# Tile-by-tile first products and a split MLP norm in a fused local-attention and MLP kernel

## The chip, the cores and the metric

The kernel runs on one core of a Trainium2 chip. The metric is the device time of one launch in microseconds. TensorE is PE (its weight loads are PEld), VectorE is DVE, ScalarE is ACT, GpSimd is POOL, and SyncE is SP, which here only issues DMAs. ACT and POOL issue some DMAs too.

## What is computed

The input is one sequence of 2048 rows of 512 features in bf16. It is normalised, goes through an attention with 32 heads of 16 features, in which each row sees eight earlier rows at a distance of two, and through an MLP block with shifted features. Their product is added to the input. Cut to its core:

```python
xn = layernorm(x)
# branch A: q, k, v = split(xn @ wqkv); row i sees rows i, i-2, ..., i-14
s  = concat_heads(softmax(q . k[i - 2w] * 16 ** -0.5, over w = 0..7) . v[i - 2w]) @ wo
# branch B: D = 512, F = 1376
h  = gelu(layernorm(xn) @ w1)            # features in four groups of 128,
hs = shift_rows(h, +1, -1, +2, -2) @ w2  # each group shifted by its own number of rows
x1 = xn + hs
b  = x1 + gelu(layernorm(x1) @ w3) @ w4
out = x + s * silu(b)
```

## The kernel before

**Layout.** Rows are split by parity, p = 0 for the even rows and p = 1 for the odd ones, so that "every second row" becomes "neighbouring rows". Each parity has 1024 rows, in two chunks of 512: chunks 0 and 1 are the even rows, 2 and 3 the odd ones. A chunk is four tiles of 128 rows. `xn[p]` holds rows on partitions, `xnT[p]` features on partitions, which is what the products need.

**Order.** The whole program is written out by hand from line 760 on, under a manual schedule: every engine takes its instructions in the order of the source lines, and waits in that order. So the place of a call in the list sets its place in five queues at once, and an instruction that waits holds back all that are behind it on its engine.

**The head** (lines 763 to 849). SP loads chunk 0 tile by tile, then the q and k weights in two DMAs (lines 140 and 141, 512 KB each), then chunk 1, `w1`, chunks 2 and 3, `wv` and `w2`. For chunk 0 each tile goes through

- `ln_first` (304): statistics on DVE (`bn_stats`, `bn_aggr`, an addition of eps), and the inverse root as a power on POOL (315),
- `first_n` (317): the normalisation on DVE,
- `first_t` (324): four PE transposes into PSUM and a copy by ACT to `xnT`.

`qk_pair(c, a, halves)` (423) makes 256 of the q and k features of a chunk in one double bank of PSUM, which ACT copies out. For chunk 0 the first three pairs run in two halves of 256 rows: the first half of each between the transposes, the second halves later. `warm` (173) is a product without use that keeps PE running.

The second norm of a chunk (branch B normalises the already normalised rows) is not computed on the rows: `ln_again` (361) works out one factor per row from the first norm's variance, with four to six small instructions, the last of them a power on POOL. `stage_r` (402) spreads the factors over the partitions with PE and ACT for chunks 0 and 3; for chunks 1 and 2 `row_turn` and `row_fill` do it with a DVE transpose and two DMAs. `stage_m` (412) multiplies `xnT` by them on DVE, and `stage_w1` (457) forms the products with `w1`, with a gelu on ACT. `ln_stats` (298) and `ln_norm` (330) are the first norm of chunks 1 to 3: statistics and normalisation on DVE, roots on POOL (279). Chunk 1 is transposed by PE (`stage_t`, 377), chunk 2 by a store and a transposing DMA (`turn_dma`, 389), chunk 3 by PE.

The attention mask is built meanwhile out of small tables: `mask_tables`, `mask_coefs` and `mask_poly` on POOL, `mask_hot`, `mask_edge`, `mask_full` and `mask_fill` on DVE. `v_ones` (271) fills the column of ones that gives the softmax its sums, on POOL. `spread` (256) moves the rows of each head to where the score products want them, in DMAs of 16 partitions; for p = 0 on SP's queue.

**The attention stretch** (lines 851 to 942). Eight units of up to 128 query rows for p = 0, later nine for p = 1. `attend(n)` (919) puts scores, exponentials, weighted sums, q and k products of chunks 2 and 3, and `w2` products (`w2_tile`) together, and then runs the list `late[n]`. These lists hold, in order of being appended:

- `ln3_stats`, `ln3_norm`, `ln3_turn` (496 to 519): the norm ahead of `w3` of a chunk: statistics and normalisation on DVE, roots on POOL, a store to DRAM and a transposing DMA back, both on SP. `ln3_norm(c, a, b)` takes tiles a to b, and stores when b reaches the end of the chunk. Chunk 0 has its norm in `late[3]`, chunk 1 in `late[6]`.
- `normalise_dn`, `normalise_mid`, `normalise_rr` (675 to 708): the softmax's sums come back from DRAM, DVE takes the reciprocal, SP writes it out and reads it back spread over the partitions.
- `pack` (681): eight DMAs of POOL's queue that bring the weighted sums to where `wo` wants them.
- `spread(1, 0, CUT, nc.gpsimd, (w,))`: the head-row moves of the odd rows, eight DMAs of POOL's queue for the keys (w = 0) in `late[3]` and eight for the queries (w = 1) in `late[5]`.

**After it** come the `w3` products of all four chunks (lines 944 to 975), then the nine units of p = 1 with the `w4` products, and the output rows.

Of the kernel before, what the change touches and what calls it, by code (L numbers as in the profile page):

```python
# [15 lines left out]
def kernel(  # L16
# [14 lines left out]
    nc = tc.nc  # L31
    P = 128
    S = 2048
    D = 512
# [4 lines left out]
    ND = D // P  # L39
# [4 lines left out]
    CH = 512  # L44
# [86 lines left out]
    for c in range(NCH):  # L131
        p, k = c // 2, c % 2
        n = 1 if c == 0 else 2
        for t0 in range(k * TPC, (k + 1) * TPC, n):
            nc.sync.dma_start(
                out=xn[p][:, t0 : t0 + n, :],
                in_=xv[p, t0 * P : (t0 + n) * P, :].rearrange("(i q) d -> q i d", q=P),
            )
        if c == 0:
            nc.sync.dma_start(out=wqk_sb[:, :, 0:D], in_=wqkv_v[:, :, 0:D])  # L140
            nc.sync.dma_start(out=wqk_sb[:, :, D : 2 * D], in_=wqkv_v[:, :, D : 2 * D])
        if c == 1:
            nc.sync.dma_start(out=w1_sb, in_=B_w1.rearrange("(dt q) n -> q dt n", q=P))
    wv_sb = const.tile([P, ND, D], BF16, name="wv_sb")
    nc.sync.dma_start(out=wv_sb, in_=wqkv_v[:, :, 2 * D : 3 * D])
    nc.sync.dma_start(out=w2_sb, in_=B_w2.rearrange("(g q) n -> q g n", q=P))
    nc.scalar.preload_act_table_set("gelu_apprx_tanh_and_others")

    def load_w3():
        nc.sync.dma_start(out=w3_sb, in_=B_w3.rearrange("(dt q) f -> q dt f", q=P))  # L150
# [22 lines left out]
    def warm(n):  # L173
        for _ in range(n):
            cnt["wm"] = cnt.get("wm", 0) + 1
            nc.tensor.matmul(
                wm[:, cnt["wm"] % 2, :], lhsT=ones_bf[:], rhs=ones_bf.unsqueeze(1).to_broadcast([P, TPC, P]),
                start=True, stop=True,
            )
# [31 lines left out]
    def mask_coefs():  # L211
        gp = nc.gpsimd
        gp.tensor_scalar(out=co[:, 0:3], in0=hot[:, 0:3], scalar1=-PEN, scalar2=None, op0=ALU.mult)
        gp.tensor_scalar(
            out=co[:, 1:2], in0=co[:, 1:2], scalar1=-2.0, scalar2=co[:, 0:1], op0=ALU.mult, op1=ALU.subtract
        )
        gp.tensor_tensor(out=co[:, 2:3], in0=co[:, 2:3], in1=co[:, 0:1], op=ALU.add)
        gp.tensor_tensor(out=co[:, 3:4], in0=hot[:, 1:2], in1=hot[:, 2:3], op=ALU.add)

    def mask_poly(w):  # L220
        gp = nc.gpsimd
        c, g = tab[:, w, 0:64], gk[:, w, :]
        f2, f1, f0 = (co[:, 0:1], co[:, 1:2], co[:, 2:3]) if w == 0 else (hot[:, 2:3], co[:, 3:4], hot[:, 0:1])
        gp.tensor_scalar(out=g, in0=c, scalar1=f2, scalar2=f1, op0=ALU.mult, op1=ALU.add)
        gp.tensor_tensor(out=g, in0=g, in1=c, op=ALU.mult)
        gp.tensor_scalar(out=g, in0=g, scalar1=f0, scalar2=None, op0=ALU.add)
# [44 lines left out]
    def v_ones():  # L271
        for va in v_aug:
            nc.gpsimd.memset(va[:, :, DH : 2 * DH], 2.0)
# [24 lines left out]
    def ln_stats(c, lo=0, hi=TPC):  # L298
        p, k = c // 2, c % 2
        lns.setdefault(c, []).append((lo, hi, *layer_stats(xn[p][:, k * TPC : (k + 1) * TPC, :], "l1", lo, hi)))  # L300
# [3 lines left out]
    def ln_first(j):  # L304
        if not first:
            first["st"] = small.tile([P, TPC, nc.vector.BN_STATS_DIM], F32, name="l0s", tag="l0s", bufs=1)
            first["mv"] = small.tile([P, TPC, nc.vector.BN_AGGR_DIM], F32, name="l0m", tag="l0m", bufs=1)
            first["r"] = small.tile([P, TPC], F32, name="l0r", tag="l0r", bufs=1)
            lns[0] = [(0, TPC, first["mv"], first["r"])]
        st, mv, rstd = first["st"], first["mv"], first["r"]  # L310
        nc.vector.bn_stats(out=st[:, j, :], in_=xn[0][:, j, :])  # L311
        nc.vector.bn_aggr(out=mv[:, j, :], in_=st[:, j, :])
        r = rstd[:, j : j + 1]
        nc.vector.tensor_scalar(out=r, in0=mv[:, j, 1:2], scalar1=EPS, scalar2=None, op0=ALU.add)
        nc.gpsimd.tensor_tensor(out=r, in0=r, in1=nhalf[:, 0:1], op=ALU.pow)  # L315
# [8 lines left out]
    def first_t(j):  # L324
        pt = pst("wb"[j % 2], "tr_ps").bitcast(BF16)[:, 0, 0:CH].rearrange("p (a q) -> p a q", a=ND)
        for dt in range(ND):
            nc.tensor.transpose(pt[:, dt, :], xn[0][:, j, dt * P : (dt + 1) * P], ident[:])
        nc.scalar.copy(out=xnT[0][:, :, j * P : (j + 1) * P], in_=pt)
# [32 lines left out]
    def ln_again(c):  # L361
        r2 = small.tile([P, TPC], F32, name="r2", tag="r2")
        eng = nc.vector if c >= 2 else nc.gpsimd
        for lo, hi, mv, rstd in lns[c]:
            r = r2[:, lo:hi]
            eng.tensor_tensor(out=r, in0=rstd, in1=rstd, op=ALU.mult)
            eng.tensor_tensor(out=r, in0=r, in1=mv[:, :, 1], op=ALU.mult)
        eng.tensor_scalar(out=r2, in0=r2, scalar1=EPS, scalar2=None, op0=ALU.add)
        if c in (1, 2):
            r2b = r2w[:, :, 0]  # L370
        else:
            r2b = small.tile([P, TPC], BF16, name="r2b", tag="r2b")
        with nc.allow_low_precision("bf16 factors"):
            nc.gpsimd.tensor_tensor(out=r2b, in0=r2, in1=nhalf, op=ALU.pow)
        r2s[c] = r2b
# [26 lines left out]
    def stage_r(c):  # L402
        rp = psb("rrep_ps")
        r2 = r2s.pop(c)
        for j in range(TPC):
            nc.tensor.matmul(
                rp[:, j * P : (j + 1) * P], lhsT=r2[:, j : j + 1].to_broadcast([P, P]), rhs=ident[:],
                start=True, stop=True,
            )
        nc.scalar.copy(out=xn2T[c][:, ND - 1, :], in_=rp)  # L410

    def stage_m(c):
        p, k = c // 2, c % 2
        cs = slice(k * CH, (k + 1) * CH)
        rrep = xn2T[c][:, ND - 1, :]
        nc.vector.tensor_tensor(
            out=xn2T[c], in0=xnT[p][:, :, cs], in1=rrep.unsqueeze(1).to_broadcast([P, ND, CH]), op=ALU.mult
        )
# [4 lines left out]
    def qk_pair(c, a, halves=1):  # L423
        p, k = c // 2, c % 2
        pt = psa("qk_ps")
        w = CH // halves

        def part(hh):
            for b in range(2):
                nt = 2 * a + b  # L430
                for dt in range(ND):
                    nc.tensor.matmul(  # L432
                        pt[:, b, hh * w : (hh + 1) * w], lhsT=wqk_sb[:, dt, nt * P : (nt + 1) * P],
                        rhs=xnT[p][:, dt, k * CH + hh * w : k * CH + (hh + 1) * w],
                        start=(dt == 0), stop=(dt == ND - 1),
                    )
            if hh == halves - 1:
                dst, n0 = qk_dst(p, 2 * a)
                nc.scalar.copy(out=dst[:, n0 : n0 + 2, k * CH : (k + 1) * CH], in_=pt)  # L439
                if c == 1:  # L440
                    nc.scalar.copy(out=dst[:, n0 : n0 + 2, M:X], in_=pt[:, :, CH - DW : CH])

        return [lambda hh=hh: part(hh) for hh in range(halves)]

    def qk_one(c, nt):
        p, k = c // 2, c % 2
# [71 lines left out]
    def ln3_turn(c):  # L518
        nc.sync.dma_start_transpose(out=x1nT[c], in_=x1n_dram[c * CH : (c + 1) * CH, :])
# [243 lines left out]
    mask_tables()  # L763
    mask_hot()
    ln_first(0)
    ln_first(1)
    mask_coefs()
    first_n(0)
    first_t(0)
    warm(1)  # L770
    first_n(1)
    first_t(1)
    warm(1)
    ln_first(2)
    mask_poly(0)
    parts = [qk_pair(0, a, 2) for a in range(3)]
    parts[0][0]()
    ln_first(3)
    first_n(2)
    first_t(2)  # L780
    parts[1][0]()
    mask_edge()
    first_n(3)
    first_t(3)
    parts[2][0]()
    ln_again(0)
    mask_poly(1)
    ln_stats(1, 0, 2)
    ln_stats(1, 2, 4)
    ln_again(1)  # L790
    v_ones()
    parts[0][1]()
    stage_r(0)
    stage_m(0)
    ln_norm(1)
    parts[1][1]()
    parts[2][1]()
    qk_pair(0, 3)[0]()
    ln_stats(2, 0, 2)
    stage_w1(0, 0)  # L800
# [6 lines left out]
    ln_norm(2)  # L807
    turn = turn_dma(2)
    ln_again(2)
    stage_w1(0, 1)  # L810
    mask_full(1)
    row_turn(2)
# [62 lines left out]
    st3(3, 4)  # L875
    st3(4, 5, 6)
    st3(5, 7)
    late[6] += [lambda: ln3_norm(1), lambda: normalise_dn(0, 1), lambda: ln3_turn(1)]

    w4s = [w4_tile(t) for t in range(S // P)]  # L880
    fill = {0: (0, 1), 1: (2,), 3: (3,), 4: (4,), 5: (5,), 7: (6,), 8: (7,)}
# [22 lines left out]
    for n, p, r in ((3, 0, 0), (6, 0, 1), (N1 + 3, 1, 0), (N1 + 6, 1, 1)):  # L904
        if (p, r) != (0, 1):
            late[n].append(lambda p=p, r=r: pack(p, r))
        if p:
            late[n].append(lambda p=p, r=r: normalise_dn(p, r))
        if (p, r) != (0, 1):
            late[n + 2].append(lambda p=p, r=r: normalise_mid(p, r))  # L910
            late[n + 2].append(lambda p=p, r=r: normalise_rr(p, r))
    late[N1 + 7].append(lambda: normalise_end(1, 0))
    CUT = 480
    for w in range(2):
        late[3 + 2 * w].append(lambda w=w: spread(1, 0, CUT, nc.gpsimd, (w,)))

    prev = None

# [130 lines left out]
```

The softmax here doesn't subtract the row's maximum and nothing guards it: scores larger than these inputs give would overflow.

## Time and profile before

| what | value |
|---|---|
| median of 7 runs (lowest to highest) | 203.66 us (203.51 to 203.74) |
| the profiled execution | 203.65 us |
| its span, first to last instruction | 201.9 us, granted TensorE clock 0.996 |
| PE busy | 193.5 us, 96% of the span |
| DVE busy | 134.2 us, 66% |
| ACT busy | 131.3 us, 65% |
| POOL busy | 73.5 us, 36% |
| bytes moved by DMA | 27.17 MB, mean 135 GB/s |
| chain that ended last | PE 90%, DVE 3%, POOL 2%, issue 1%, DMA 1% |

The span leaves out 1.75 us of the execution's 203.65 us, ahead of the first instruction and after the last. A timeline line gives start and length in microseconds, engine, line of the source, operation, what is written and read, and in brackets how long the engine was idle before it and what ended that. Lines of the chain of work have start, length, engine, tile and line. PE's ends are modelled and longer than its spacing, so neighbouring records overlap; spacing is read from starts. A share of busy time near 1 in a stretch says that PE was the limit there, or that it was just in step with what was.

### The profile page before, as it was taken

To read this page: it belongs to the slowest core of one execution; us is meant where nothing else is said; L and a number is where in the kernel's file an instruction comes from. 1 tells how busy PE (TensorE), PEld (TensorE's weight loads), DVE (VectorE), ACT (ScalarE), POOL (GpSimd) and SP (SyncE) were. 2 spreads that over 40 slices of the span, in tenths; PEclk is the share of its full clock that TensorE was granted. 3 is DMA by queue.
4 is the path that set the end of the run, shared out by engine and by line. 5 is a ranking of instruction groups with operands and counts; after the bars stand their busy time and mean duration, and the time that the engine had idled before them with its cause. 6 is when DMAs were issued, how large, how long until landed. Compare 5 with 4: busy or idle time off the path is not lost.

```text
span 201.9 us, 4886 instructions
## 1 busy us (share of the span) xinstructions
PE 193.5 (96%) x1939; PEld 95.0 (47%) x1967; DVE 134.2 (66%) x263; ACT 131.3 (65%) x155; POOL 73.5 (36%) x146
## 2 busy tenths in 40 slices
PE   7899999999999999999999999999999999999991
PEld 2475445444444444444444444444554444444460
DVE  5788889735298988888610510278577958676683
ACT  2367665859988888896665566998788879212120
POOL 4789516200023095887760000004830590700000
PEclk9999999999999999999999999999999999999998
DMA  5993256367750089498989667890230051564221
GB/s 134 352 351 104 71 147 128 63 103 115 150 211 5 27 184 146 68 256 140 209 241 212 226 121 109 214 350 26 36 51 5 8 134 31 110 175 158 79 78 54
DMA packets 33734, 27.17 MB, mean 135 GB/s; under 512 B 14720, under 2 KB 31624, under 8 KB 33712
## 3 DMA queue, kind: packets, MB, share of 16 engines
q1 hardware_dynamic: 31520, 23.64, 46.3%
q0 software_dynamic: 2048, 3.09, 8.7%
q8 instruction: 15, 0.25, 0.5%
q10 hardware_dynamic: 144, 0.13, 0.2%
q14 instruction: 7, 0.06, 0.1%
HBM read 12.82 MB, written 4.98 MB: 88 GB/s over the span
## 4 chain that ended last, share of the span: by engine, by line
PE 90%; DVE 3%; POOL 2%; issue 1%; DMA 1%; ACT 0%; DVEq 0%
PE w_ps L567 18%; PE w_ps L530 17%; PE qk_ps L432 8%; PE v_ps L596 8%; PE w_ps L488 7%; PE s_ps L621 7%; PE w_ps L465 7%; PE wo_ps L742 6%; PE o_ps L644 5%; PE qk_ps L450 4%; PE w_ps L547 1%; DMA arena<-in_A_x_dram 1%; DVE l0s L311 1%; POOL l0r L315 1%; PE tr_ps L384 1%
## 5 line engine op out<-in xcount | busy, mean ns | idle before, releaser
L626 ACT ACTIVATE arena<-s_ps 128x960 bf16<-128x960 f32 (+1 forms) x68 | 62.7, 975 | 12.4 <-PE s_ps L621 12.3
L567 PE MATMUL w_ps<-arena 128*128 128x512 bf16 (+1 forms) x164 | 39.3, 368 | 0.5 <-issue 0.2
L534 ACT ACTIVATE arena<-w_ps 128x1024 bf16<-128x1024 f32 x20 | 20.5, 1023 | 13.3 <-PE w_ps L530 13.3
L686 POOL DMA_DIRECT2D arena<-orw x48 | 24.8, 524 | 5.8 <-DVE orw L656 5.8
L567 PEld LDWEIGHTS <-arena 128*128 128x128 bf16 x187 | 17.6, 98 | 18.9
L752 POOL TENSOR_TENSOR arena<-arena 128x512 bf16<-128x512 bf16 x6 | 7.7, 1302 | 46.3 <-DVE arena L751 46.3
L530 PEld LDWEIGHTS <-arena 128*128 128x128 bf16 x160 | 15.5, 98 | 19.2 <-issue 0.8
L573 DVE TENSOR_TENSOR arena<-w_ps,arena 128x512 bf16<-128x512 f32 (+1 forms) x17 | 11.2, 660 | 14.7 <-PE w_ps L567 14.7
L432 PE MATMUL qk_ps<-arena 128*128 128x512 bf16 (+1 forms) x109 | 20.2, 332 | 0.7 <-DMA arena<-in_A_wqkv_dram 0.5
L656 DVE CAST orw<-o_ps 128x960 bf16<-128x960 f32 (+1 forms) x17 | 19.7, 1157 | 1.5 <-PE o_ps L644 1.3
L601 DVE CAST v_aug<-v_ps 128x512 bf16<-128x512 f32 x17 | 11.7, 690 | 10.2 <-PE v_ps L596 10.2
L582 ACT ACTIVATE arena<-arena 128x512 bf16<-128x512 bf16 (+1 forms) x9 | 5.2, 583 | 20.4 <-DVE arena L573 20.4
L530 PE MATMUL w_ps<-arena 128*128 128x512 bf16 x78 | 17.7, 379 | 0.2
L596 PE MATMUL v_ps<-wv_sb,arena 128*128 128x512 bf16 x68 | 17.5, 380 | 0.0
L530 PE MATMUL w_ps<-arena,arena 128*128 128x512 bf16 x78 | 17.3, 379 | 0.1
L621 PEld LDWEIGHTS <-arena 32*128 32x128 bf16 x544 | 10.2, 92 | 14.5 <-issue 14.4
L621 PE MATMUL s_ps<-arena 32*128 32x120 bf16 (+1 forms) x544 | 15.9, 214 | 0.0
L488 PE MATMUL w_ps<-arena 128*128 128x512 bf16 x64 | 15.3, 380 | 0.0
L492 DVE TENSOR_TENSOR arena<-w_ps,arena 128x512 bf16<-128x512 f32 x16 | 10.4, 684 | 7.2 <-PE w_ps L488 7.2
L439 ACT CAST arena<-qk_ps 128x1024 bf16<-128x1024 f32 x11 | 11.1, 1020 | 6.0 <-PE qk_ps L432 6.0
L432 PEld LDWEIGHTS <-arena 128*128 128x128 bf16 x112 | 10.7, 98 | 8.4 <-DMA arena<-in_A_wqkv_dram 0.9
L280 POOL TENSOR_SCALAR l3r<-l3m 128x1 f32<-128x1 f32 (+2 forms) x11 | 2.6, 234 | 33.1 <-DVE l3m L289 33.1
(108 smaller groups left out, 275.1 us busy)
## 6 DMA issues: line engine op xcount, KB each, us to landing
x1n_dram<-arena SPq DMA_DIRECT2D x5, 512.0 KB, 3.9
arena<-in_A_x_dram SPq DMA_DIRECT2D x4, 512.0 KB, 5.5
arena<-in_A_x_dram SPq DMA_DIRECT2D x6, 256.0 KB, 7.2
out_dram<-arena SPq DMA_DIRECT2D x6, 256.0 KB, 2.1
arena<-in_B_w_dram SPq DMA_DIRECT2D x1, 1376.0 KB, 6.6
arena<-in_B_w_dram SPq DMA_DIRECT2D x1, 1280.0 KB
arena<-arena SPq DMA_DIRECT2D x16, 72.0 KB, 2.5
arena<-arena SPq DMA_DIRECT2D x16, 68.0 KB, 2.7
```

The costliest lines, as they stand in the source:

```text
L432: nc.tensor.matmul(pt[:, b, hh * w : (hh + 1) * w], lhsT=wqk_sb[:, dt, nt * P : (nt + 1) * P], rhs=xnT[p][:, dt, k * CH + hh * w : k * CH ...
L465: nc.tensor.matmul(pt[:, b, :], lhsT=w1_sb[:, dt, g * P : (g + 1) * P], rhs=xn2T[c][:, dt, :], start=(dt == 0), stop=(dt == ND - 1),)
L488: nc.tensor.matmul(pt, lhsT=w2_src(p, g, m0), rhs=w2_sb[:, g, :], start=(g == 0), stop=(g == ND - 1))
L530: nc.tensor.matmul(pt[:, ft % 2, :], lhsT=w3_sb[:, dt, ft * P : (ft + 1) * P], rhs=x1nT[c][:, dt, :], start=(dt == 0), stop=(dt == ND - 1),)
L534: nc.scalar.activation(h3(c, 2 * a, 2), pt, AF.Gelu_apprx_tanh)
L567: nc.tensor.matmul(pt, lhsT=h3(c, ft, 1)[:, 0, jj * P : (jj + 1) * P], rhs=w, start=(ft == 0), stop=(ft == NF - 1),)
L596: nc.tensor.matmul(vp[:nk, :], lhsT=xnT[p][:, dt, k0 : k0 + nk], rhs=wv_sb[:, dt, :], start=(dt == 0), stop=(dt == ND - 1),)
L621: nc.tensor.matmul(st[:nk, b, i * nq : (i + 1) * nq], lhsT=kT[e][r : r + 32, dt, k0 : k0 + nk], rhs=qT[e][r : r + 32, dt, q0 : q0 + nq], s ...
L626: nc.scalar.activation(prv[:nk, 2 * h : 2 * h + 2], st[:nk, :, 0 : 4 * nq], AF.Exp, scale=SCALE)
L656: nc.vector.tensor_copy(out=orw[p, r][:, :, :, q0 - ra : q0 - ra + nq], in_=op[:, :, 0 : 4 * nq].rearrange("p j (s q) -> p j s q", q=nq),)
L686: nc.gpsimd.dma_start(out=oT[p][DH * hh : DH * (hh + 1), :, ra : ra + rw], in_=orw[p, r][32 * cg : 32 * cg + DH, jj],)
L742: nc.tensor.matmul(pt, lhsT=oT[p][:, dt, i * P : (i + 1) * P], rhs=wo_sb[:, dt, ds], start=(dt == 0), stop=(dt == ND - 1),)
```

## The change

There are two parts.

**The head.** The first half of the q and k weights is issued on ACT's queue, behind the load of ACT's first function table, and no longer on SP's. `ln_first` is cut into `first_s` (the statistics) and `first_a` (aggregate, addition, root), so that DVE can take the next tile's statistics ahead of this tile's normalisation, and the aggregate behind it. The first three q and k pairs of chunk 0 run in four parts of 128 rows, one part behind each tile's transposes, in place of two halves. On POOL `mask_coefs` moves from before the first normalisation to behind the first roots of chunk 1, `mask_poly(0)` and `mask_poly(1)` to behind `ln_again(1)`, and `v_ones` from there to behind `ln_again(2)`. One of the two single warm products goes. The statistics of chunk 1 and `stage_m(0)` come in another order with the last parts of the products.

**The attention stretch.** The norm ahead of `w3` of chunk 1 runs in two parts, two tiles in `late[5]` and two in `late[6]`. The reciprocals of the first run of sums (`normalise_mid(0, 0)`, `normalise_rr(0, 0)`) move from `late[5]` to `late[6]`, around `normalise_dn(0, 1)` and `ln3_turn(1)`; those of the second run stay where they were, after the stretch. The head-row moves of the keys go from `late[3]` to `late[5]`, ahead of those of the queries and behind the statistics of the chunk's last tile.

```diff
         if c == 0:
-            nc.sync.dma_start(out=wqk_sb[:, :, 0:D], in_=wqkv_v[:, :, 0:D])
             nc.sync.dma_start(out=wqk_sb[:, :, D : 2 * D], in_=wqkv_v[:, :, D : 2 * D])
...
     nc.scalar.preload_act_table_set("gelu_apprx_tanh_and_others")
+    nc.scalar.dma_start(out=wqk_sb[:, :, 0:D], in_=wqkv_v[:, :, 0:D])
...
             lns[0] = [(0, TPC, first["mv"], first["r"])]
+        first_s(j)
+        first_a(j)
+
+    def first_s(j):
+        nc.vector.bn_stats(out=first["st"][:, j, :], in_=xn[0][:, j, :])
+
+    def first_a(j):
         st, mv, rstd = first["st"], first["mv"], first["r"]
-        nc.vector.bn_stats(out=st[:, j, :], in_=xn[0][:, j, :])
         nc.vector.bn_aggr(out=mv[:, j, :], in_=st[:, j, :])
...
+    def qk_first(a):
+        pt = psa("qk_ps")
+
+        def part(lo, hi):
+            for b in range(2):
+                nt = 2 * a + b
+                for dt in range(ND):
+                    nc.tensor.matmul(
+                        pt[:, b, lo:hi], lhsT=wqk_sb[:, dt, nt * P : (nt + 1) * P],
+                        rhs=xnT[0][:, dt, lo:hi], start=(dt == 0), stop=(dt == ND - 1),
+                    )
+            if hi == CH:
+                dst, n0 = qk_dst(0, 2 * a)
+                nc.scalar.copy(out=dst[:, n0 : n0 + 2, 0:CH], in_=pt)
+
+        return part
...
     mask_hot()
     ln_first(0)
-    ln_first(1)
-    mask_coefs()
+    first_s(1)
     first_n(0)
     first_t(0)
+    first_a(1)
+    first_s(2)
     warm(1)
     first_n(1)
     first_t(1)
-    warm(1)
-    ln_first(2)
-    mask_poly(0)
-    parts = [qk_pair(0, a, 2) for a in range(3)]
-    parts[0][0]()
-    ln_first(3)
+    first_a(2)
+    qa = [qk_first(a) for a in range(3)]
+    for a in range(3):
+        qa[a](0, P)
+    first_s(3)
     first_n(2)
     first_t(2)
-    parts[1][0]()
+    for a in range(3):
+        qa[a](P, 2 * P)
+    first_a(3)
     mask_edge()
     first_n(3)
     first_t(3)
-    parts[2][0]()
+    for a in range(3):
+        qa[a](2 * P, 3 * P)
     ln_again(0)
+    ln_stats(1, 0, 2)
+    mask_coefs()
+    qa[0](3 * P, CH)
+    stage_r(0)
+    for a in (1, 2):
+        qa[a](3 * P, CH)
+    ln_stats(1, 2, 4)
+    stage_m(0)
+    ln_again(1)
+    mask_poly(0)
     mask_poly(1)
-    ln_stats(1, 0, 2)
-    ln_stats(1, 2, 4)
-    ln_again(1)
-    v_ones()
-    parts[0][1]()
-    stage_r(0)
-    stage_m(0)
     ln_norm(1)
-    parts[1][1]()
-    parts[2][1]()
     qk_pair(0, 3)[0]()
...
     ln_again(2)
+    v_ones()
     stage_w1(0, 1)
...
-    late[6] += [lambda: ln3_norm(1), lambda: normalise_dn(0, 1), lambda: ln3_turn(1)]
+    late[5].append(lambda: ln3_norm(1, 0, 2))
+    late[6] += [
+        lambda: ln3_norm(1, 2, 4), lambda: normalise_mid(0, 0), lambda: normalise_dn(0, 1),
+        lambda: ln3_turn(1), lambda: normalise_rr(0, 0),
+    ]
...
-        if (p, r) != (0, 1):
+        if p:
             late[n + 2].append(lambda p=p, r=r: normalise_mid(p, r))
             late[n + 2].append(lambda p=p, r=r: normalise_rr(p, r))
...
     for w in range(2):
-        late[3 + 2 * w].append(lambda w=w: spread(1, 0, CUT, nc.gpsimd, (w,)))
+        late[5].append(lambda w=w: spread(1, 0, CUT, nc.gpsimd, (w,)))
```

## The prediction

> **What bounds the kernel now.** I read the chain of work that ended last, then busy time by stretch, then the timeline of POOL, DVE and PE up to 37 us, then waits and DMA issues. The chain, with start, length, engine and line:
>
> ```profile
> 7.34 0.58 POOL l0r L315
> 7.91 0.40 POOL arena L224
> ...
> 8.85 0.47 POOL arena L226
> 9.32 0.55 POOL l0r L315
> 9.90 0.42 DVE arena L319
> 10.37 0.40 PE tr_ps L327 x4
> 10.77 1.75 PE qk_ps L432 x16
> ...
> 16.21 1.73 PE w_ps L465 x8
> ```
>
> Until 10.4 us the norm of chunk 0 leads, with three mask instructions of POOL in its way; from there on PE is on the chain almost without a break. The stretches (from:to, length, busy time and count of PE, PEld, DVE, ACT, POOL, clock, DMA share, GB/s) agree:
>
> ```profile
> 7.40:10.40 3.00, 2.35 (x21) 1.66 (x22) 2.35 (x10) 0.58 (x1) 2.65 (x7) 1.00 1.08 348
> 20.40:27.40 7.00, 6.95 (x32) 3.05 (x32) 5.67 (x17) 4.57 (x7) 2.96 (x4) 1.00 0.29 94
> 45.90:86.80 40.90, 40.35 (x606) 19.88 (x614) 32.16 (x56) 34.53 (x43) 16.37 (x36) 1.00 0.58 115
> ```
>
> PE idles 0.65 us in 7.4:10.4 and then hardly at all. A microsecond won at the start reaches the end only if nothing that PE needs later stays where it was. So I looked for operands that arrive with no room to spare:
>
> ```profile
> 14.08 1.23 DVE L416 TENSOR_TENSOR arena<-arena 128x2048 bf16<-128x2048 bf16 x1 [0.57 <-ACT arena L410]
> 14.20 1.19 POOL L280 TENSOR_SCALAR l1r<-l1m 128x2 f32<-128x2 f32 x1
> ...
> 21.45 0.57 POOL L280 TENSOR_SCALAR l1r<-l1m 128x2 f32<-128x2 f32 x1 [0.78 <-DVE l1m L289]
> 22.10 0.73 POOL L281 TENSOR_TENSOR l1r<-l1r,nhalf 128x2 f32<-128x2 f32 x1
> 22.87 0.74 DVE L335 TENSOR_SCALAR arena<-arena,l1m,l1r 128x512 bf16<-128x512 bf16 x2 [0.28 <-POOL l1r L281]
> 24.42 1.39 POOL L374 TENSOR_TENSOR r2w<-r,nhalf 128x4 bf16<-128x4 f32 x1 [1.59 <-DVE r L368]
> 25.85 0.31 DVE L345 STREAM_TRANSPOSE r2t<-r2w 128x128 bf16<-128x128 bf16 x1 [0.91 <-POOL r2w L374]
> 26.08 1.18 DVE L416 TENSOR_TENSOR arena<-arena 128x2048 bf16<-128x2048 bf16 x1
> 27.41 3.61 PE L465 MATMUL w_ps<-arena 128*128 128x512 bf16 x16
> 34.47 2.30 POOL L374 TENSOR_TENSOR r2b<-r,nhalf 128x4 bf16<-128x4 f32 x1 [1.59 <-DVE r L368]
> 36.82 0.32 PEld L406 LDWEIGHTS <-r2b 128*128 128x128 bf16 x4 [0.22 <-POOL r2b L374]
> ```
>
> This is the **second chain**. POOL's last root for chunk 2 ends at 22.10 + 0.73 = 22.83; DVE normalises, POOL takes r2w (to 25.81), DVE turns it and, queued behind that, runs stage_m(1), 26.08 to 27.26; PE takes its first w1 product of chunk 1 at 27.41. DVE then runs without a gap to 36.7, POOL's r2b ends under it at 36.77, and PE loads it at 36.82 after a wait. So room is 0.15 us at 27.4 and none at 36.8: **after 37 us PE moves only as far as the end of POOL's root at 22.83 moves.**
>
> [...] L280 under L416 took 1.19 us, alone 0.22 (19.65). [...] 348 GB/s in 7.4:10.4 from SP alone. [...] Here 16 transposes of 128 columns, each with its weights (L384), take 0.89 us, 56 ns each; I use 56. [...] The load here takes 1.28 us (0.72 to 2.00); whether a DMA behind it waits is not in this trace.
>
> **First part, the head.** First weights on ACT's queue: SP's issue at 2.59 (0.43 us) goes; ACT issues at about 0.75, or at 2.0 if the load holds it. PE waited for these weights until 7.46 (0.9 us); DMA moved only 116 GB/s in 4:5, so an earlier issue fills a hole. They then land at 5.5 to 6.5. The second half, issued at 3.06 with 5.8 us to landing, came at 8.9; with the hole filled, 7.3 to 8.2. The cost: 512 KB now share the engines with the first x tile (2.93). Bounds 0 (issue at 2.0) and 0.4 us; I take 0.15, call it d.
>
> DVE's new order, with the durations above (statistics 0.61 to 0.70, aggregate 0.19, add 0.16, root on POOL 0.58 to 0.67, normalise 0.41): n0 starts at 4.75, when POOL's root ends (4.72), not at 5.06; n1 at 6.23; n2 at 7.72 (was 8.18); n3 behind mask_edge (0.88) at 9.43 (was 9.90). All plus d.
>
> PE: transposes of tile 1 end near 6.9. Tile by tile means 24 products of 128 columns, 24 x 0.056 = 1.33 us a tile: 6.9 to 8.25; transposes 0.22; second tile to 9.8; transposes to 10.1; third to 11.4; qa[0] of the fourth 0.44, stage_r 0.22, the rest 0.87; qk_pair(0,3) 1.73, to 14.8. r2b is there at 11.35 (n3's root, and 1.93 for ln_again(0)). On ACT qa[0]'s copy (1.0) and the copy of rrep (0.59) end at 13.5, stage_m(0) (1.23) at 14.8. So w1 of chunk 0 starts at 14.85 against 16.05: **1.2 us earlier** for PE, less what the second half of the weights, needed at 7.8, comes late (0 to 0.4). One warm product (0.4) goes; PE was idle there.
>
> **First part, POOL.** From 11.47 (statistics of the first two tiles of chunk 1 end 2.02 after n3 starts): roots 1.03, mask_coefs 0.97 (new here), roots 1.03, ln_again(1) 2.5, mask_poly 1.38 and 1.30 (new here, v_ones' 0.99 gone to behind r2w), roots for chunk 2 1.00 and 1.03: 10.2, to 21.7 with no block. But stage_m(0), now at 13.55, meets the roots of chunk 1: 0.85 to 1.1 us. mask_full(0), at 20.2, meets mask_poly(1) or a root: 0 to 0.35 (it cost L280 0.35 at 21.45). That ends **POOL at 22.65 to 23.1, against 22.83**; most likely 22.7, and with d 22.85. In the old order 0.78 us of POOL's time here was waiting for statistics; it now works, but on 3.65 us of mask work that used to lie between 5.8 and 13.2, in place of 0.99 us of ones. DVE, in order, waits behind it at L335, and stage_m(1) and PE behind that.
>
> v_ones lands in POOL's idle 4.36 us before 30.18; its first user is the weighted sum at 52.7. SP's later issues come 0.45 us earlier, at a full DMA: nothing.
>
> **Sum.** PE is ready for w1 of chunk 1 at 26.2 and waits for stage_m(1), about 1.1 us; at 36.8 it stands where POOL's root stands, 22.85 - 22.83 = +0.02. If the cover went (chain free of POOL) it would be -1.2. The transposed chunk 2 moves with the same chain and stays ahead of its use at 31.73.
>
> **Second part, the attention stretch.** POOL's eight head-row moves for keys (75.46 to 82.37) stood ahead of three roots at 82.39, and DVE's ln3_norm(1) waited for them at 84.18 and 85.06. Now the roots come right after the packing, near 75.5; half the norm at 79, half near 83.5; the store goes from 85.50 to about 84, the transposing DMA from 90.96 to about 87.5. It lands 7.7 us after its issue: 98.7 before, about 95 after. Its user starts at 100.37 and had no wait: worth 0. Moved with it: a reciprocal (0.70) on DVE from 78.97, where 0.67 us were idle, to behind the norm; its store and the broadcast read on SP behind the norm's store and transpose, from 83.60 to about 89, used by DVE at 93.92. If that is late, DVE waits there, and the next PE user is chunk 3, far behind. The key moves go to 80 to 88.6, used at 124.9. In 45.9:86.8 PE idles 0.55 us in all, mostly the last exponentials at 85.77, which this doesn't touch. Bounds -0.1 and +0.1; I take 0.
>
> The profiled run took 203.65 us with a span of 201.9; the median of seven is 203.66. Added: 203.7.
>
> **The rivals.** *Slower*: the same POOL queue. Each block not counted (d at 0.4, mask_full at its 0.35, the roots of chunk 1 caught a second time, 0.3) goes to the end whole once the root for chunk 2 ends past 22.83; from 23.25 on it can be measured. At 23.4 it gives 204.25. For it: nothing on POOL has room from 11.5 to 23. Against: DVE's statistics, most of the time there, don't block POOL. *Faster*: stage_m(0) or the roots fall so that they don't meet, and POOL ends at 21.7 to 22.2: 202.6 to 203.05. For it: 0.78 us of old waiting is turned to work. Against: stage_m has to lie somewhere in POOL's busy stretch. *It doesn't do what it says*: the weights on ACT's queue land no earlier. PE then loses up to 1 us of its 1.2, and the end is the same, 203.7, since the wait at 27 shrinks by as much; this lies inside the forecast.
>
> **How the numbers follow.** No change that can be measured, 0.54; slower 0.29 (sums of small terms err upward more easily); faster 0.17. A difference of 0.2% (0.4 us) is about what a measurement of this kernel can tell from none. The range 203.0 to 204.4 holds the first case and most of both others.
>
> **What would show it.** Right: PE at its first w1 product near 15 us, not 16; an idle PE of about 1 us just before w1 of chunk 1 near 27.3; L335 of chunk 2 waiting for POOL; the transposing DMA of chunk 1 near 87 and no other stretch changed. Wrong: no gap near 27; POOL's root of chunk 2 before 22.2 or past 23.3; [...] the first x tile landing past 3.3; PE waiting on DMA past 8.8.

## The result and the profile after

| kernel | median us (lowest to highest, runs) | profiled execution, span | ratio to before, 95% interval |
|---|---|---|---|
| before, same chip | 203.66 (203.51 to 207.79, 32 runs, all but one below 204.8) | 203.65, 201.9 | 1 |
| after | 205.2 (204.34 to 205.55, 13 runs) | 205.55, 203.8 | 1.0069 [1.0058, 1.0081] |

The change makes the kernel 1.5 us slower in the medians; the profiled executions differ by 1.9 us. The forecast was 203.7, in a range of 203.0 to 204.4, and no change that can be measured. The page of after has PE busy for 194.7 us (193.5 before). Of the 1.9 us of span, 1.2 are longer work of PE and 0.7 are more idle time.

The chain of work that ended last, at the start of after (start, length, engine, tile, line):

```profile
1.21 4.68 DMA arena<-in_A_x_dram
5.91 0.69 DVE l0s L314
...
7.87 0.42 DVE arena L325
8.34 0.40 PE tr_ps L333 x4
8.74 2.38 PE qk_ps L458 x24
...
11.55 1.72 PE qk_ps L458 x24
...
18.27 1.84 PE w_ps L488 x8
```

Two things are new. The chain now begins with a transfer of x, and what it releases is the *second* tile's statistics, at 5.91. And the 24 products of 128 columns take 2.38 and 1.72 us, 99 and 72 ns each, where the prediction had 56. The stretches of after (from:to, length, busy time and count of PE, PEld, DVE, ACT, POOL, clock, DMA share, GB/s) show the second; the last two are among those that the prediction read in before:

```profile
5.39:8.81 3.42, 1.18 (x15) 0.75 (x15) 2.75 (x9) 0.62 (x2) 0.73 (x2) 1.00 1.09 353
8.81:12.22 3.41, 3.41 (x36) 3.41 (x34) 3.21 (x12) 1.14 (x2) 2.27 (x6) 0.50 1.10 350
...
7.40:10.40 3.00, 2.24 (x25) 2.06 (x25) 2.74 (x11) 1.17 (x2) 1.39 (x3) 0.73 1.10 351
45.90:86.80 40.90, 40.43 (x592) 19.91 (x600) 30.65 (x54) 34.33 (x42) 14.75 (x32) 1.00 0.57 108
```

The first two are cut where the trace's record of the granted clock steps. From 5.39 to 8.81 PE works for 1.18 us of 3.4; from 8.81 to 12.22 it gets half of the full clock, then the full clock again until 203.37. In 7.4:10.4, which this half stretch covers in part, the mean was 1.00 before and is 0.73 now. The attention stretch is as it was.

One line of the timeline of before, the statistics of the second tile, which follow the first's without a wait:

```profile
3.97 0.68 DVE L311 BATCH_NORM_STATS2 l0s<-arena 128x6 f32<-128x512 bf16 x1
```

The timeline of after, at the places that the prediction named:

```profile
3.28 0.69 DVE L314 BATCH_NORM_STATS2 l0s<-arena 128x6 f32<-128x512 bf16 x1 [1.39 <-DMA arena<-in_A_x_dram]
5.91 0.69 DVE L314 BATCH_NORM_STATS2 l0s<-arena 128x6 f32<-128x512 bf16 x1 [1.53 <-DMA arena<-in_A_x_dram]
...
18.22 1.89 PE L488 MATMUL w_ps<-arena 128*128 128x512 bf16 x8
23.63 0.57 POOL L280 TENSOR_SCALAR l1r<-l1m 128x2 f32<-128x2 f32 x1 [0.81 <-DVE l1m L289]
24.28 0.73 POOL L281 TENSOR_TENSOR l1r<-l1r,nhalf 128x2 f32<-128x2 f32 x1
29.59 2.75 PE L488 MATMUL w_ps<-arena 128*128 128x512 bf16 x12
38.99 0.34 PEld L412 LDWEIGHTS <-r2b 128*128 128x128 bf16 x4 [0.20 <-POOL r2b L380]
```

The first tile's statistics start at 3.28 (2.96 before), the second's at 5.91 (3.97) after a wait of 1.53. w1 of chunk 0 starts at 18.22 (16.05 before), w1 of chunk 1 at 29.59 (27.41), 11.37 us later as in before (11.36): PE has no gap between them. POOL's root ends at 25.01 (22.83), after a wait for DVE, so POOL's queue is not the limit here. r2b is loaded at 38.99 (36.82). From there on every stage stands 2.17 us later, until the last microsecond gives 0.23 back (below): 1.94, the difference of the profiled spans (1.9).

### The profile page after: what moved, and what is told of

Its sections match the earlier page's. It is cut to its first block, busy times and chain, and to the rows that moved or that the text cites. A ratio compares the mean times of both kernels' runs of the same rounds, so it can differ in the third digit from the quotient of the medians.

```text
span 203.8 us, 4981 instructions
## 1 busy us (share of the span) xinstructions
PE 194.7 (96%) x1986; PEld 97.2 (48%) x2014; DVE 133.8 (66%) x263; ACT 131.3 (64%) x155; POOL 73.5 (36%) x146
## 4 chain that ended last, share of the span: by engine, by line
PE 92%; DMA 2%; DVE 2%; issue 1%; ACT 0%; POOL 0%; SPq 0%; DVEq 0%
PE w_ps L590 18%; PE w_ps L553 17%; PE v_ps L619 8%; PE w_ps L511 7%; PE w_ps L488 7%; PE qk_ps L438 7%; PE s_ps L644 7%; PE wo_ps L765 6%; PE o_ps L667 4%; PE qk_ps L473 4%; PE qk_ps L458 3%; DMA arena<-in_A_x_dram 2%; PE w_ps L570 1%; PE tr_ps L390 1%; DVE arena L770 1%
## 5 line engine op out<-in xcount | busy, mean ns | idle before, releaser
L557 ACT ACTIVATE arena<-w_ps 128x1024 bf16<-128x1024 f32 x20 | 20.5, 1024 | 13.3 <-PE w_ps L553 13.3
L590 PEld LDWEIGHTS <-arena 128*128 128x128 bf16 x187 | 17.6, 98 | 18.9
L553 PEld LDWEIGHTS <-arena 128*128 128x128 bf16 x160 | 15.5, 98 | 19.2 <-issue 0.8
L553 PE MATMUL w_ps<-arena 128*128 128x512 bf16 x78 | 17.7, 379 | 0.2
L280 POOL TENSOR_SCALAR l3r<-l3m 128x1 f32<-128x1 f32 (+2 forms) x11 | 2.7, 241 | 38.3 <-DVE l3m L289 38.2
L511 PE MATMUL w_ps<-arena 128*128 128x512 bf16 x64 | 15.3, 380 | 0.0
L515 DVE TENSOR_TENSOR arena<-w_ps,arena 128x512 bf16<-128x512 f32 x16 | 10.4, 683 | 7.2 <-PE w_ps L511 7.2
L438 PE MATMUL qk_ps<-arena 128*128 128x512 bf16 x61 | 14.5, 379 | 0.2
L488 PE MATMUL w_ps<-arena 128*128 128x512 bf16 x63 | 14.6, 379 | 0.0
L492 ACT ACTIVATE arena<-w_ps 128x1024 bf16<-128x1024 f32 x8 | 8.2, 1029 | 5.2 <-PE w_ps L488 5.2
```

What stands on the lines that cost most here:

```text
L438: nc.tensor.matmul(pt[:, b, hh * w : (hh + 1) * w], lhsT=wqk_sb[:, dt, nt * P : (nt + 1) * P], rhs=xnT[p][:, dt, k * CH + hh * w : k * CH ...
L488: nc.tensor.matmul(pt[:, b, :], lhsT=w1_sb[:, dt, g * P : (g + 1) * P], rhs=xn2T[c][:, dt, :], start=(dt == 0), stop=(dt == ND - 1),)
L511: nc.tensor.matmul(pt, lhsT=w2_src(p, g, m0), rhs=w2_sb[:, g, :], start=(g == 0), stop=(g == ND - 1))
L553: nc.tensor.matmul(pt[:, ft % 2, :], lhsT=w3_sb[:, dt, ft * P : (ft + 1) * P], rhs=x1nT[c][:, dt, :], start=(dt == 0), stop=(dt == ND - 1),)
L557: nc.scalar.activation(h3(c, 2 * a, 2), pt, AF.Gelu_apprx_tanh)
L590: nc.tensor.matmul(pt, lhsT=h3(c, ft, 1)[:, 0, jj * P : (jj + 1) * P], rhs=w, start=(ft == 0), stop=(ft == NF - 1),)
```

## Experiments

All ratios are to the kernel before, timed on the same chip beside each batch (medians 203.62 to 203.69).

| run | median us (range, runs) | ratio [95%] |
|---|---|---|
| e1_wq_on_sp | 203.07 (202.67 to 204.54, 16) | 0.9978 [0.9967, 0.9990] |
| e2_only_queue | 205.25 (205.12 to 205.37, 4) | 1.0080 [1.0066, 1.0093] |
| e3_only_part2 | 203.41 (203.27 to 203.51, 13) | 0.9988 [0.9980, 0.9996] |
| e4_x_shared | 203.49 (203.23 to 204.21, 13) | 0.9997 [0.9989, 1.0005] |
| e5_one_dve_more | 203.46 (203.34 to 204.79, 21) | 0.9994 [0.9986, 1.0002] |
| e6_warm_in_gap | 204.42 (204.34 to 204.72, 5) | 1.0036 [1.0024, 1.0049] |
| e7_mask_behind | 203.04 (202.72 to 205.44, 22) | 0.9976 [0.9957, 0.9995] |
| e8_stats_behind | 204.92 (204.20 to 204.98, 6) | 1.0049 [1.0033, 1.0065] |
| e9_masks_split | 203.24 (203.19 to 203.55, 15) | 0.9978 [0.9969, 0.9987] |
| e10_masks_one_queue | 203.12 (202.48 to 205.64, 22) | 0.9971 [0.9957, 0.9984] |

**Theory.** The weights on ACT's queue take the DMA engines from tiles 2 to 4 of chunk 0, and the loss goes to the end. (The prediction and the expectations count the tiles from 0: their tile 1 is the second tile.) **Rivals.** The new order of the head (tile by tile, masks on POOL) costs the time; or the second part does.

**1. The change without its queue** (after, weights back on SP):

```diff
         if c == 0:
+            nc.sync.dma_start(out=wqk_sb[:, :, 0:D], in_=wqkv_v[:, :, 0:D])
...
-    nc.scalar.dma_start(out=wqk_sb[:, :, 0:D], in_=wqkv_v[:, :, 0:D])
```

> The changed kernel with one thing undone: the first half of the q and k weights is issued by SP again, between the last x tile and the second half. Theory A (the 512 KB of weights on ACT's queue share the DMA engines with the first x tiles, tile 1 lands at 5.9 us and not at 3.3, and DVE, in order, can't normalise tile 0 before): x tiles land by 2.9 to 4.4, n0 starts near 4.75, the weights land at 7.4 and 8.9 as before the change; POOL's last root for chunk 2 ends near 22.7 and the time falls to 203.3 to 203.9. Theory B (the order in tiles costs it: 128-column products, the mask work on POOL): it stays at 204.8 to 205.4. Theory C (the second part costs it): also 204.8 to 205.4.

Measured 203.07, ratio 0.9978: one line of the change holds the whole loss, and the rest is worth a gain of 0.2%. The timeline of this run:

```profile
8.77 0.62 PE L458 MATMUL qk_ps<-arena 128*128 128x128 bf16 x8 [0.46 <-DMA arena<-in_A_wqkv_dram]
...
14.56 1.26 POOL L373 TENSOR_TENSOR r<-r,l1m 128x2 f32<-128x2 f32 x1
...
21.32 0.56 POOL L280 TENSOR_SCALAR l1r<-l1m 128x2 f32<-128x2 f32 x1
21.96 0.73 POOL L281 TENSOR_TENSOR l1r<-l1r,nhalf 128x2 f32<-128x2 f32 x1
36.67 0.34 PEld L412 LDWEIGHTS <-r2b 128*128 128x128 bf16 x4 [0.20 <-POOL r2b L380]
```

PE begins its products at 7.24, 1.3 us earlier than in after, and at full clock, though it waits 0.46 us for the second half of the weights. The prediction's account of POOL can be read here. stage_m(0), from 14.54, met an addition of ln_again(1): 1.26 us against 0.20 (at 15.96 in after), 1.06 longer (predicted 0.85 to 1.1). mask_full(0), at 21.14, met L280: 0.56 against 0.22 (at 21.79 in after), 0.34 longer (predicted 0 to 0.35). The root ends at 22.69 (predicted 22.65 to 23.1), 0.14 earlier than in before, and r2b is loaded 0.15 earlier. With the tail's 0.23 (run 3) that is 0.38 of the gain: 0.4 in the spans, 0.55 in the medians. The profiled execution, 203.35, lies above the median, and where the other 0.15 comes from no trace shows.

**2. The queue alone** (before, with the two lines of the first diff the other way round):

> The kernel before with one line of the change: the first half of the q and k weights is issued by ACT behind its table load. Theory A: tile 1 lands near 5.9, the second normalisation comes 1.9 to 2.2 us later than before, and so does all that follows: 205.2 to 205.9. Theory B and C: 203.2 to 203.8, the weights even come earlier.

205.25, ratio 1.0080: the full loss without any other part of the change. That refutes the rivals as the cause of the loss. The granted clock is 0.50 from 7.70 to 11.11 here too. But one of the four executions, with a mean clock of 1.0, took 205.29 all the same, so in this order of the head the slower clock cost nothing that this one execution shows, and the late tiles make the loss.

**3. The second part alone** (before, with the two last hunks of the diff):

> The kernel before with the second part alone: norm of chunk 1 in two halves, reciprocals in late[6], head-row moves of the keys in late[5]. Theories A and B: 203.5 to 203.8, the transposing DMA of chunk 1 near 87 and no change on PE. Theory C: above 204.2.

203.41, ratio 0.9988: a gain of 0.2 us, not a loss. The transposing DMA of chunk 1 goes out at 89.64 (90.96 before), not at 87.5: the store ahead of it, at 84.02, takes 5.6 us. But PE has no wait less for it. The chain of this run and that of before part only in the last microseconds. Before:

```profile
197.65 0.40 issue
198.05 0.43 DVE arena L747
```

With the second part:

```profile
197.72 0.17 issue
197.89 0.42 DVE arena L747
```

"issue" is time in which DVE waited for nothing that is shown. Before the last pair of instructions it is 0.40 us in before and 0.17 here.

**4. Tiles on two queues, weights behind them** (run 1, with the odd tiles of chunk 0 on ACT's queue):

```diff
-            nc.sync.dma_start(
+            (nc.scalar if c == 0 and t0 % 2 else nc.sync).dma_start(
                 out=xn[p][:, t0 : t0 + n, :],
```

> The changed kernel with the weights back on SP and the first four x tiles shared out, tiles 0 and 2 by SP, 1 and 3 by ACT. Theory A: all four x tiles are issued by 1.7 and land by 2.9 to 4.0, the weights land near 6.5 and 8.0, about 0.9 us earlier than before the change; PE's first w1 product comes near 15. If POOL's roots for chunk 2 are the second bound (near 22.7), the time is 203.2 to 203.8 all the same; if they are not, 202.5 to 203.0. Theory B: 204.5 to 205.4.

203.49, ratio 0.9997. The head is the fastest of all: w1 of chunk 0 starts at 15.48, 0.57 us earlier than before. The timeline of PE's weight loads shows where that goes:

```profile
27.55 3.15 PEld L488 LDWEIGHTS <-arena 128*128 128x128 bf16 x16 [1.12 <-PE qk_ps L438]
...
36.97 0.34 PEld L412 LDWEIGHTS <-r2b 128*128 128x128 bf16 x4 [0.20 <-POOL r2b L380]
```

A gap of 1.12 us opens ahead of w1 of chunk 1, POOL's root ends at 23.00 (0.17 later than before), and r2b is loaded at 36.97 (0.15 later). This is the second chain, as predicted: the head's gain is cut off at 27 us, and the rest moves as the root moves.

**5. One DVE instruction more, for nothing** (before, with a second clear of r2w at the start):

```diff
     nc.vector.memset(r2w[:], 0.0)
+    nc.vector.memset(r2w[:], 0.0)
```

> The kernel before with one more tiny DVE instruction at the very start, where DVE waits anyway (the zeroing of r2w twice); nothing is left out. Theory D (the 0.2 us that the second part won alone is no work saved: the traces with it have one DVE instruction more, and the last product with x waits 0.17 us and not 0.40 behind the instruction before it): 203.35 to 203.5, with the short wait at the end. Rival (the second part really relieves something): 203.6 to 203.7, and the wait at the end stays 0.40.

203.46, ratio 0.9994 [0.9986, 1.0002]; the interval reaches to no change, but the trace decides: the last L747 starts before the recorded end of the instruction ahead of it, as in run 3, not 0.14 us after it. So it is in after and in all experiments but run 2. The trace holds 325 records of DVE's queue for before and run 2, 326 for every other kernel. The 0.23 us at the tail are no saved work of the second part: one instruction more at the start of DVE's queue has the same effect. Why it has, no run shows.

The profiled execution of this run, a late one (204.61), shows what the second part could be worth after all. In its timeline chunk 1's w3 products wait for the transposed rows:

```profile
97.26 3.78 PEld L531 LDWEIGHTS <-arena 128*128 128x128 bf16 x19 [1.53 <-DMA arena<-x1n_dram]
```

They were ready to start at 97.26 - 1.53 = 95.73. So the user of chunk 1's rows starts near 95.7, not at 100.37. By the traces' landing events the rows came at 95.42 in before, at 97.22 in this late execution, and at 93.85 with the second part alone. Without the second part (before, beside the experiments, and this run), 9 of 137 executions are more than 0.8 us above their medians at a mean clock of 0.994 or more; with it (runs 1, 3, 4, 7, 9, 10) none of 101 is. It fits that the second part takes away these late executions. That is argued from three traces and these counts, not shown.

**6. Warm products in the gap** (after, with products without use where PE waits for tiles 1 and 2):

```diff
     first_n(0)
+    warm(4)
     first_t(0)
...
-    warm(1)
+    warm(3)
```

> The changed kernel, weights on ACT's queue as it has them, with four warm products ahead of the first transposes and three in place of one behind them, so that PE doesn't idle while x tile 1 is late. Theory E (half of the loss is the clock: after 1.5 us of idle PE ran the 128-column products at 99 and 72 ns and not at 56): the products take 56 to 60 ns, and the time falls to 203.9 to 204.5. Rival (the late tile alone sets the time): 205.0 to 205.6, whatever the clock.

204.42, ratio 1.0036. The stretch that had half the clock in after:

```profile
8.81:12.22 3.41, 3.41 (x65) 3.41 (x62) 3.17 (x13) 1.46 (x3) 2.27 (x6) 1.00 1.10 348
```

65 matmuls fit where 36 did. With seven warm products instead of one and the second tile nearly as late as in after (its statistics start at 5.64, not 5.91), 0.8 us of the 1.5 come back in the medians (1.2 in the profiled spans, 203.8 to 202.6). What stays is the tiles' share: the root now ends at 23.83 on a POOL chain that shows no wait ahead of it (L281 at 21.65 took 1.16 us, 0.73 at 23.10), 1.0 late, less the 0.23 of the tail, 0.77 (measured 0.73). In after itself two of the 13 executions kept a mean clock of 1.0 and took 204.34 and 204.94, the others 204.80 to 205.55.

**7. Can the second chain be shortened?** Run 4 with mask_poly behind the roots of chunk 2, and mask_full(0) and mask_full(1) each moved back:

```diff
-    mask_poly(0)
-    mask_poly(1)
     ln_norm(1)
...
-    mask_full(0)
+    mask_poly(0)
     ln_norm(2)
     turn = turn_dma(2)
     ln_again(2)
+    mask_poly(1)
     v_ones()
     stage_w1(0, 1)
-    mask_full(1)
+    mask_full(0)
...
+    mask_full(1)
     mask_fill(0, (1,))
```

> The kernel of e4 with the mask work put behind the roots of chunk 2: mask_poly(0) behind them, mask_poly(1) behind ln_again(2), mask_full(0) where mask_full(1) was, mask_full(1) ahead of the filling of the queries. If POOL's roots for chunk 2 hold PE at 27.5 (PE idles 1.1 us there in e4): they end near 21.4, the gap closes, and the time is 202.3 to 202.8. Rival (PE's wait there has another cause, or the moved mask_full(1) costs what is won): 203.2 to 203.6.

203.04, ratio 0.9976: a gain, half of what was expected. The gap at 27 is closed and the root ends at 22.27, 0.56 earlier, but r2b is loaded at 36.68, only 0.14 earlier. The rest is lost on the way, a little at each step: stage_m(1) starts at 25.72, 0.36 earlier; DVE's work from there to r2b takes 0.09 us more; and POOL's power for r2b takes 2.42 us from 34.20 on, not 2.30, and now runs under stage_m(2) and mask_full(1) on DVE, back to back.

**8. The second tile's statistics behind the first tile's normalisation** (after, to see whether DVE's order makes the gap):

```diff
-    first_s(1)
     first_n(0)
     first_t(0)
+    first_s(1)
```

> The changed kernel with the statistics of x tile 1 behind the normalisation of tile 0 on DVE, weights on ACT's queue. If DVE's order is what turns the late tile into a loss: n0 at 5.1 and not 6.5, PE's transposes of tile 0 at 5.5, time 203.8 to 204.6. If the late landing itself is (n1 can't come before about 7.5 in either order): 204.8 to 205.4.

204.92, ratio 1.0049. The first tile is transposed at 5.40, not 6.97, but the second only at 7.76 (8.34 in after), PE idles for 1.76 us ahead of it, and the clock is 0.50 from 8.35 to 11.76. Holding the first tile back behind statistics whose data were late cost 0.3 us; the landing of the second makes the rest. Two of its six executions kept a mean clock of 0.995 or more and took 204.20 and 204.24; the four with 0.989 to 0.991 took 204.87 to 204.98. Within this kernel the price of the clock is 0.7 us.

**9 and 10. Both repairs together** (run 4 with other places for the masks): mask_full(1) back in its place, mask_poly(0) in POOL's wait for statistics, mask_full(0) between the halves of the norm of chunk 2, and the second half of the weights in two transfers; in run 10 all x tiles on SP as well.

```diff
-    mask_poly(0)
-    mask_poly(1)
     ln_norm(1)
...
     ln_stats(2, 0, 2)
+    mask_poly(0)
     stage_w1(0, 0)
...
-    mask_full(0)
-    ln_norm(2)
+    mask_poly(1)
+    ln_norm(2, slice(0, 1))
+    mask_full(0)
+    ln_norm(2, slice(1, 2))
...
-            nc.sync.dma_start(out=wqk_sb[:, :, D : 2 * D], in_=wqkv_v[:, :, D : 2 * D])
+            nc.sync.dma_start(out=wqk_sb[:, :, D : D + D // 2], in_=wqkv_v[:, :, D : D + D // 2])
+            nc.sync.dma_start(out=wqk_sb[:, :, D + D // 2 : 2 * D], in_=wqkv_v[:, :, D + D // 2 : 2 * D])
```

> The run with the mask work behind the roots ended its second chain only 0.14 us earlier, since DVE met the moved mask_full(1) ahead of r2b, and its products waited for the second half of the weights until 8.6. Here mask_full(1) is back where it was, mask_poly(0) lies in POOL's wait for statistics (19.6 to 21.2), mask_full(0) between the two halves of the norm of chunk 2, and the second half of the weights comes in two transfers of 256 KB, the needed one first. Theory (the end moves with POOL's root for chunk 2, then with r2b): first products of tile 0 without a wait near 8, root's end 22.0 to 22.4, r2b loaded by PE at 36.1 to 36.5, 202.4 to 202.9 us. Rival (another operand takes the place of r2b, DVE itself being full from 27 to 36): r2b at 36.6 to 36.8 and 203.0 to 203.2 us.

> The same order of mask work and the same split of the second half of the weights, with all tiles and weights on SP's queue. Theory (the head's transfers set only when PE starts, and what PE has ready is cut off at the second chain): w1 of chunk 0 starts some 0.3 us later than with the tiles on two queues, but first x tile lands 0.3 us earlier, so DVE and POOL run ahead; root's end 21.9 to 22.3 and 202.4 to 202.9 us, the same as the other within 0.2. Rival (the landing of the weights decides): 0.3 us later than the other.

203.24 and 203.12, ratios 0.9978 and 0.9971: faster than both kernels, and no better than runs 1 and 7. Run 9, in which PE does not wait for weights, is the steadiest (15 executions within 0.36 us); runs 1, 7 and 10 have a few late ones, from 204.36 to 205.64, all with a mean clock of 0.987 to 0.990. The theory's 202.4 to 202.9 did not come. The timeline of run 10 shows why:

```profile
21.39 1.34 POOL L282 TENSOR_TENSOR l1r<-l1r,nhalf 128x2 f32<-128x2 f32 x1
...
21.48 0.68 DVE L242 TENSOR_TENSOR arena<-arena,edge 128x512 bf16<-128x512 bf16 x1
```

mask_full(0), put where DVE would have waited for the root, runs beside that root, which takes 1.34 us against 0.72 (at 18.78). The root ends at 22.73 and r2b is loaded at 36.91: back where it was. The profiled execution took 203.45, so the trace of run 10 does not show where the median's other 0.3 us come from.

## Why the prediction was wrong

**The step that failed** is in the part on the head: "The cost: 512 KB now share the engines with the first x tile (2.93). Bounds 0 (issue at 2.0) and 0.4 us; I take 0.15, call it d", followed by "All plus d". The first tile was inside its bounds (0.32). But ACT issued the weights at 0.75, behind the first tile (0.73) and ahead of the second (1.21), and the other three tiles were given the first one's delay. The second tile's statistics start at 5.91; the prediction has the first tile normalised at 4.75 plus d and the second at 6.23 plus d, 6.6 at the latest. They start at 6.52 (behind the second's statistics, though the first tile's root had ended at 5.04) and 7.87. From issue to landing the second tile took 4.7 us, 2.1 before. The issue at 0.75 is at the early end of what was named, as the lines of ACT show:

```profile
0.72 1.28 ACT L146 ACT_TABLE_LOAD   x1 [0.72 <-PEq L1065]
0.75 0.45 ACTq L147 DMA_DIRECT2D arena<-in_A_wqkv_dram  x1
```

Issued so early, the weights landed ahead of these tiles: at 5.51 by the trace's landing events, with the second tile at 5.88 and the fourth at 6.61, where the fourth had landed at 4.38 before. The prediction said that an earlier issue "fills a hole", with 116 GB/s in 4:5. It filled it, but with bytes that pushed the tiles into the hole; the tiles are needed first.

A count for all four tiles would have priced it: an estimate, from 350 GB/s (the stretches above), is that 512 KB of weights take 1.5 us from the tiles with which they share. The view of the DMA queues shows when each queue was served (q1 is SP's queue, q10 ACT's; packets of about 1 KB, MB, share of the engines). From 3.0 to 4.4 us, then from 5.1 to 6.7:

```profile
q10 hardware_dynamic: 331, 0.34, 92.5%
...
q1 hardware_dynamic: 597, 0.57, 107.4%
```

Between 2.94 and 4.42 not one packet of SP's queue starts: the first tile was served, then most of the weights, then the other tiles, in the order of issue. This pause is 1.5 of the 2.2 us by which the fourth tile is late. For the rest there is one sign: from 1.5 to 3.6 us the DMA moved 124 GB/s, 225 in before; why, no run shows. So the prediction's account of the second issuer, SP's issue of 0.43 us saved and 0.15 us (d) lost, falls short here: the earlier issue also changed which transfer was served first. No run tried the weights on ACT's queue behind the issue of the last tile (2.13).

**The price of 56 ns** failed too, for a reason that the prediction left out. In runs 1 and 6, 24 such products take 1.34 us from their start to the next transposes' (9.45 to 10.79, 8.31 to 9.65): 56 ns each, as taken. In after they took 99 and 72. The late tiles let PE idle, and the granted clock fell to 0.50: in after and in runs 2 and 8 it was half for one stretch of 3.41 us at the head. The stretch of the same length ahead of it was not idle; PE worked there for 1.18, 1.29 and 1.54 us, and its longest pauses in after were 1.5 and 0.8. Counted in the same steps, the emptiest stretches that left the clock full held 1.81 (run 10), 1.83 (run 4) and 1.94 us (run 1). So in the heads of these six traces the half clock came behind stretches with 1.54 us of work or less in 3.41, and behind none with 1.81 or more. The steps begin at other places in each execution (5.39 in after, 4.29 in run 2, 4.93 in run 8); it fits that of one kernel some executions lose the clock and others do not, but only one trace of each was kept. The step "One warm product (0.4) goes; PE was idle there" cost that at nothing; run 6 puts seven in place of one and wins 0.8 us. That is about half of the loss in after; in run 2, the old order of the head, the one execution with the full clock won nothing.

**The second chain** was right, and the runs show it as far as the root sets the time. Root's end and r2b's load, against before: -0.14 and -0.15 (run 1), +0.17 and +0.15 (run 4), +2.18 and +2.17 (after, where PE itself was as late). In run 4, 0.57 us won in the head end in the gap at 27. In run 7 the rule has its limit: -0.56 at the root, -0.14 at r2b, since 0.42 us are lost in small steps between the two.

**w1 of chunk 0 at 14.85** was too early even without the late tiles: 15.48 in run 4, 15.91 in run 1, 1.06 late. Of this, 0.46 us is a wait for the second half of the weights, which landed at 8.72, past the end of the range given (8.2). Run 4 suggests that it cost nothing at the end, since the chain at 27 cuts off what PE wins.

**The second part at 0** was right in what it does for PE in an undisturbed execution. "Its user starts at 100.37 and had no wait" was misread: the chain merges 49 products to one piece, and chunk 1's products begin inside the piece that starts at 89.58. The transfer was misjudged too: 7.7 us from issue to landing are chunk 0's; chunk 1's took 4.5 and landed at 95.42, not 98.7. In before the rows were ready some 0.3 us ahead of their user. And the tail's 0.23 us was in no view that I had read as changeable.

**The rivals.** The slower one put the loss on POOL's queue; in after POOL waits for DVE, and the loss begins at the tiles. That DVE's statistics don't block POOL can be read in before: the L280 at 19.65, which the prediction calls alone, ran beside statistics (from 19.70) and took 0.22 us, against 1.19 beside stage_m(0). The third one, that the weights land no earlier, was the wrong way round: they landed two microseconds earlier, and that was the harm. None of the three reached past 204.4. With the queue left alone, the rest of the change gives 203.07, at the low end of the range.

## What to carry to other kernels

Here a transfer that was issued earlier on a second queue was paid for by the transfers issued behind it (the fourth tile landed 2.2 us later), not by the one under way alone (0.32): list all that are due before such a transfer, with their users, and issue the bulky one behind them (203.07 us in run 1, 203.49 in run 4). Where late data open pauses on PE, price a slower clock behind the pause too (24 products took 2.38 us in after, most of them at 0.50, and 1.34 in run 6 at 1.00), and keep warm products there until the data are known to come in time (seven in place of one won 0.8 us in run 6). A gain in one stage was worth no more than the next operand's lead (in run 4, 0.57 us won at w1 of chunk 0 and r2b loaded 0.15 later); find that operand first, and when it is shortened, look which vector instruction now lies beside it (in run 10 the root beside mask_full(0) took 1.34 us, not 0.72).

## What the runs showed that was not expected

- ACT's DMA issue did not wait for the table load ahead of it: issued at 0.75, with the load from 0.72 to 2.00.
- At the head of after and of runs 2 and 8, a stretch of 3.41 us with 1.18 to 1.54 us of PE work was followed by one of the same length at half the clock; with 1.81 us and more (runs 1, 4 and 10) the clock stayed full.
- With weights and tiles on two queues, no packet of the tiles' queue started for 1.5 us, until most of the weights had been served.
- One DVE instruction of no use at the start takes the last pause on DVE from 0.40 to about 0.17 us, and with it some 0.2 us from the end.
- With mask_full(0) laid into a pause on DVE (run 10), the very POOL root for which DVE was pausing took 1.34 us, against 0.72.
